# Seven block products in place of eight for the first products of the last 768 tokens

## Chip, cores and metric

The kernel runs on one core of a Trainium2 chip. The metric is the device time of one execution in microseconds; lower is better. The core has five engines with queues of their own: TensorE (PE, its weight loads as PEld), VectorE (DVE), ScalarE (ACT), GpSimd (POOL) and SyncE (SP), which here issues the DMAs.

## What is computed

Top-32 attention for 4 batches of 8 heads over 576 tokens, then two feed-forward layers on all 2304 tokens, in fp32.

```python
scores = scale * np.matmul(q, k.transpose(0, 1, 3, 2))
kth = np.partition(scores, -top_k, axis=-1)[..., -top_k:-top_k + 1]
...
x = np.ascontiguousarray(attn_out.transpose(0, 2, 1, 3)).reshape(B * S, H * D)   # 2304 x 512
x = (lambda h: np.maximum(0.01 * h, h) @ w_out)(x @ w_in)                       # 512 -> 2048 -> 512
h = x @ moe2_w_in
g = np.where(h >= 1, h, np.where(h <= -1, 0.0, (h + 1) ** 2 / 4.0))
out = g @ moe2_w_out
```

## The kernel before

Every feed-forward product is made of three matmuls (`mm3`, lines 829 to 832): an fp32 operand is held as a rounded part and a remainder (`split`, line 397: a cast on ACT, a subtraction on POOL), and high by high, high by low and low by high are added in one PSUM bank. Weights are split once, early in the kernel, and kept in DRAM (`scr`); `load_w` (line 495) brings one 128 x 2 x 512 tile of 512 KB into one of six `ring` buffers.

The program is written as a list of operations with dependences, and `Plan` (line 79 on) puts them in order at build time: it plays the list with a cost and a priority for every operation, lets every engine take the first operation that is ready and has its buffers, and emits the instructions in that order. So each engine's order is fixed before the run. `close` (line 90) adds an operation that waits for all operations on a set of tiles and then frees their memory for others: here those of the weight preparation (`EARLY`) for those of later attention (`LATE`).

Attention goes unit by unit (`unit_out`, line 988). When a block of tokens is done, `split_x` (line 820) splits it, and `FLOW` (line 36) says which blocks go through which layer (`ffn`, line 936). The last two entries are the last 768 tokens: the two blocks of 256 of batch 3, and the 4 x 64 remainders of all batches (`"r"`, tile `xr`). For 512 tokens `hidden` (line 853) makes the first product of one chunk of 128 of the 2048 hidden values at 512 columns, and for `"r"` two chunks at 256 columns; activation and split follow; `sums` (line 886) adds the second product in banks kept for the whole layer, two steps later. In the first layer the second product has the weights as the stationary operand and tokens as columns, in the second layer the activations are stationary and the 512 outputs are the columns. TensorE's feed-forward work comes after attention's in priority, so a backlog of it remains when attention ends.

## Time and profile before

| | us |
|---|---|
| median of 3 runs | 1185.3 (1185.26 to 1187.74) |
| the profiled execution | 1185.56 |
| its span in the trace | 1183.8 |
| TensorE busy in it | 1131.7 |
| Vector, Scalar, GpSimd busy | 869.9, 843.0, 710.2 |

The span is from the first to the last instruction in the trace. Recorded durations of matmuls overlap, since they are pipelined; how fast they follow one another is read from their starts. PEclk is the granted share of TensorE's full clock. A line number can be that of a helper, so tiles are named with it: `x` are split tokens, `gt` split activations, `t` and `gr` activation buffers, `ring` weights, `bank` PSUM banks.

### The profile page before, as it was taken

How to read it: one execution, taken by the hardware profiler on the slowest of the kernel's cores; microseconds unless marked ns; L12 is line 12 of the kernel's file. 1: busy time of each engine (PE TensorE's matmuls, PEld its weight loads, DVE VectorE, ACT ScalarE, POOL GpSimd, SP SyncE). 2: the span in 40 equal slices, each digit the busy share in tenths (PEclk: the TensorE clock that was granted, in tenths of full speed). 3: DMA queues.
4: the chain of work that ended last, by engine and by line, in shares of the span. 5: the costliest groups of instructions: out<-in, count | busy, mean ns of one | idle time of the engine just before them, and what ended most of it. 6: DMA issues, size and time to landing. Idle time of an engine off the chain costs nothing.

```text
span 1183.8 us, 18889 instructions
## 1 busy us (share of the span) xinstructions
PE 1131.7 (96%) x6240; PEld 966.1 (82%) x6240; DVE 869.9 (73%) x1761; ACT 843.0 (71%) x1889; POOL 710.2 (60%) x820
## 2 busy tenths in 40 slices
PE   6778898998999999999999999999999999999998
PEld 4566697997888888888888888888888888888887
DVE  7999999997999999999999999989961000012221
ACT  6888899997999989889877999888553212142223
POOL 3445588986979878677866678768462322252221
PEclk8988999999999999999999999999999999999999
DMA  9888798589658555545555564443546343233322
GB/s 343 283 301 298 234 368 323 204 314 383 231 199 285 181 196 171 199 155 196 192 198 175 171 202 150 136 142 121 175 147 197 136 143 114 100 142 143 137 100 102
DMA packets 78322, 236.45 MB, mean 200 GB/s; under 512 B 8720, under 2 KB 21136, under 8 KB 74128
## 3 DMA queue, kind: packets, MB, share of 16 engines
q1 hardware_dynamic: 78224, 235.24, 57.4%
q8 instruction: 49, 0.80, 0.3%
q14 instruction: 49, 0.40, 0.1%
HBM read 192.22 MB, written 42.99 MB: 199 GB/s over the span
## 4 chain that ended last, share of the span: by engine, by line
PE 72%; ACT 9%; DVE 8%; POOL 7%; issue 2%; DMA 1%; SPq 0%; POOLq 0%; ACTq 0%; DVEq 0%
PE bank L830 14%; PE bank L831 14%; PE bank L832 14%; PE bank L698 5%; PE bank L902 5%; PE bank L903 5%; PE bank L904 5%; PE bank L672 5%; DVE m L618 4%; PE bank L570 3%; DVE wk L622 3%; POOL px L390 2%; ACT e L640 2%; PE bank L718 2%; POOL e L657 1%
## 5 line engine op out<-in xcount | busy, mean ns | idle before, releaser
L390 POOL TENSOR_TENSOR gt<-gr,gt 128x512 fp32r<-128x512 f32 x144 | 187.8, 1304 | 256.2 <-ACT gt L374 132.8
L618 DVE MAX8 m<-wk 128x8 f32<-128x576 f32 x432 | 309.4, 748 | 0.5
L878 DVE TENSOR_SCALAR t<-bank 128x512 f32<-128x512 f32 x72 | 49.5, 687 | 237.5 <-POOL x L390 142.7
L622 DVE MATCH_REPLACE8 wk<-m,wk 128x576 f32<-128x576 f32 x288 | 212.6, 744 | 0.0
L830 PE MATMUL bank<-x,ring 128*128 128x512 f32 (+1 forms) x568 | 207.6, 366 | 0.3 <-DVE gr L881 0.3
L832 PE MATMUL bank<-x,ring 128*128 128x512 f32 (+1 forms) x568 | 202.3, 356 | 0.0
L831 PE MATMUL bank<-x,ring 128*128 128x512 f32 (+1 forms) x568 | 202.2, 356 | 0.0
L672 PE MATMUL bank<-idt,e 128*116 128x128 f32 (+1 forms) x720 | 110.4, 281 | 16.5 <-POOL e L657 9.4
L376 ACT ACTIVATE t<-t,half 128x512 f32<-128x512 f32 x72 | 52.2, 725 | 102.1 <-DVE t L878 102.1
L390 POOL TENSOR_TENSOR pt<-ptr,pt 116x512 fp32r<-116x512 f32 (+1 forms) x96 | 106.0, 1126 | 29.4 <-ACT pt L374 21.8
L657 POOL TENSOR_SCALAR e<-e,rc 128x576 f32<-128x576 f32 x144 | 111.6, 784 | 16.0 <-DVE rc L655 14.4
L832 PEld LDWEIGHTS bank<-x,ring 128*128 128x128 f32 x568 | 107.3, 189 | 15.7
L374 ACT COPY ptr<-bank 116x512 f32<-116x512 f32 (+1 forms) x224 | 106.4, 511 | 18.4 <-PE bank L672 15.9
L672 PEld LDWEIGHTS bank<-idt,e 128*116 128x116 f32 (+1 forms) x720 | 85.9, 138 | 40.0 <-POOL e L657 17.5
L830 PEld LDWEIGHTS bank<-x,ring 128*128 128x128 f32 x568 | 107.5, 189 | 12.2 <-DVE gr L881 0.9
L376 ACT ACTIVATE gt<-bank 128x512 fp32r<-128x512 f32 x72 | 43.2, 600 | 103.4 <-PE bank L832 103.0
L831 PEld LDWEIGHTS bank<-x,ring 128*128 128x128 f32 x568 | 107.7, 190 | 10.3
L618 DVE MAX8 m<-s 128x8 f32<-128x576 f32 x144 | 104.2, 747 | 8.6 <-ACT s L374 8.4
L376 ACT ACTIVATE e<-s,nb 128x576 f32<-128x576 f32 x144 | 108.4, 777 | 1.4
L830 PE MATMUL bank<-gt,ring 128*128 128x512 f32 (+1 forms) x304 | 109.3, 360 | 0.0
L374 ACT COPY s<-bank 128x288 f32<-128x288 f32 x256 | 96.1, 403 | 17.1 <-PE bank L570 15.7
L832 PE MATMUL bank<-gt,ring 128*128 128x512 f32 (+1 forms) x304 | 106.8, 351 | 0.0
(97 smaller groups left out, 2812.4 us busy)
## 6 DMA issues: line engine op xcount, KB each, us to landing
ring<-scr SPq DMA_DIRECT2D x212, 512.0 KB, 3.5
scr<-px SPq DMA_DIRECT2D x58, 512.0 KB, 4.9
wraw<-in_moe_w_in_dram SPq DMA_DIRECT2D x16, 1024.0 KB, 7.0
wraw<-in_moe_w_out_dram SPq DMA_DIRECT2D x16, 1024.0 KB, 7.4
kraw<-in_km_dram SPq DMA_DIRECT2D x40, 288.0 KB, 4.6
vl<-in_vd_dram SPq DMA_DIRECT2D x24, 320.0 KB, 5.8
qraw<-in_qm_dram SPq DMA_DIRECT2D x24, 256.0 KB, 3.9
vl<-in_vp_dram SPq DMA_DIRECT2D x16, 320.0 KB, 3.7
```

Source lines behind the costliest of these rows:

```text
L374: nc.scalar.copy(out=out_(), in_=in_())
L376: nc.scalar.activation(out=out_(), in_=in_(), func=func, **a)
L390: lambda: nc.gpsimd.tensor_tensor(out=out_(), in0=in0(), in1=in1(), op=ALU.subtract),
L618: vec(lambda i=i, c=c, src=src: nc.vector.max(out=m()[:, i, c], in_=src()), 664, [(m, (i, r))], [src], pr)
L622: vec(lambda i=i, c=c, src=src, w=ws[i]: nc.vector.match_replace(out=w(), in_to_replace=m()[:, i, c], in_values=src(), imm_value=NEG), 720 ...
L657: P.op("P", T_NORM, lambda i=i: nc.gpsimd.tensor_scalar(out=es[i](), in0=es[i](), scalar1=rc()[:, i:i + 1], scalar2=1.0, op0=ALU.mult, op1 ...
L672: nc.tensor.transpose(ps()[0:p, i * 128:(i + 1) * 128], e()[:, cols[j]], idt())
L698: nc.tensor.matmul(out_ps()[:, 0:w], lhsT=vt()[0:p, j, :], rhs=pt()[0:p, c] if lean else pt()[0:p, part, c], start=bi == 0 and part == 0 a ...
L830: nc.tensor.matmul(ps, lhsT=wh, rhs=xh, start=first, stop=False, skip_group_check=True)
L831: nc.tensor.matmul(ps, lhsT=wh, rhs=xl, start=False, stop=False, skip_group_check=True)
L832: nc.tensor.matmul(ps, lhsT=wl, rhs=xh, start=False, stop=last, skip_group_check=True)
L902: nc.tensor.matmul(acc[z](), lhsT=gh[:, c], rhs=wo()[:, 0], start=st, stop=False)
```

## The change

The last two entries of `FLOW` are replaced by `ffn_wide`. The 768 tokens stay in one tile `xr` and are seen as two halves of 384; the 512 features as two halves of 256; the hidden chunks as pairs (even, odd). For each pair, the 2 x 2 x 2 block product of tokens, features and chunks is made in seven products instead of eight (the Winograd form): `operands` makes the seven token operands from sums and differences (four sums for each of two feature chunks, fourteen splits), once a layer; `weights` makes four sums of weight blocks for each pair (two additions on POOL, four on DVE, two splits). The results are put together in four banks: ACT copies the bank of the first product to a second bank, on which TensorE then adds further products, and DVE adds the product kept in `p5` to it twice between two of them (`both`). `bend` is the activation.

Activations of the first half of the tokens (`g0`) are split at once and go into second sums, which are issued between the products of the next pair in the numbers of `FILL`. Those of the second half (`g1`) are kept unsplit for the whole layer; `late_split` splits them later, and their second sums follow when all eight pairs are through, with the second weights loaded a second time. These late sums end with the last three pairs taken bank by bank. The matmuls of `sums` are the same as before, at 384 columns in the first layer and 512 in the second. In the second layer the first two pairs do their first two products, which need the first half of the tokens alone, ahead of the others.

A third stage of memory is opened when all attention is done (`third`): the tiles in `LAST` take the place of those in `ATT` and `LATE`, and no operation on them starts earlier. The storage of old `x` and `gt` tiles is used again for late activations and split weight sums. Costs in the planner for the new operations are separate functions (`t_aa`, `t_pp`, `t_vv`). The diff, cut:

```diff
-LATE = ("vv", "vraw", "pt", "xb", "xr")
+LATE = ("vv", "vraw", "pt", "xb")
+ATT = ("xraw", "kk", "vl", "kraw", "qraw", "qh", "s", "wk", "e", "m8", "nb", "y", "sums", "rc", "ptr")
+BYVEC = (3, 4)
+TAIL = 3
+FILL = (((0, 0, 0, 0), (2, 2, 2, 2), (2, 2, 2, 2)), ((0, 0, 0, 0), (0, 0, 0, 3), (2, 2, 2, 1)))
+L_EARLY = 1
+EARLY_AT = ((0, 6, 2, 4), (1, 0, 3, 2))
+LAST = dict(xa=1, g0=2, g1=8, t0=2, u7=1, p5=2, tsn=2, wf=2, tf=2, ring2=4, cc=2)
+WORK = dict(gd=4, ts=5)
...
+    def load_w(key, prio, tag="ring"):
...
-        wt = new("ring", [128, 2, DM], F32R)
+        wt = new(tag, [128, 2, DM], F32R)
...
+    last = ((B - 1, 0), (B - 1, 1), "r")
+    x_raw = {}
...
+    def third():
+        late.close()
+        att.close()
+        for tag in LAST:
             pools[tag] = ctx.enter_context(tc.tile_pool(name="p_" + tag, bufs=1))
...
+        def product(self, ps, o, name, begin):
+            wt, k0 = self.w[name]
+            xa = self.wide.xa
+            for k in range(2):
+                def mm(k=k):
+                    c = slice((k0 + k) * 128, (k0 + k + 1) * 128)
+                    mm3(ps()[:, 0:HW], wt()[:, 0, c], wt()[:, 1, c], xa()[:, o, 0, k], xa()[:, o, 1, k], begin and k == 0, k == 1)
+                pe(mm, 3 * t_m(HW), [ps], [(xa, ((o, k), 0)), (xa, ((o, k), 1)), wt], fprio())
+        def bend(self, e, z, src, sref, psum):
+            hi, n, L, g0, r0, g1 = -5.0, HW, self.L, self.g0, self.r0, self.g1
+            dst, dref = (lambda: r0[e](), [r0[e]]) if z == 0 else (lambda: g1()[:, e], [(g1, e)])
+            if L == 0:
+                if z == 0:
+                    slope(lambda: g0()[:, e, 0], src, t_aa(n, psum), 0.01, [(g0, (e, 0))], sref, hi)
+                slope(dst, src, t_aa(n, psum), 0.01, dref, sref, hi)
+            else:
+                act(dst, src, t_aa(n, psum), dref, sref + [half1], hi, func=ACTF.Relu, scale=0.5, bias=half1)
+                act(dst, dst, t_aa(n), dref, dref, hi, func=ACTF.Square)
+                vec(lambda: nc.vector.scalar_tensor_tensor(out=dst(), in0=src(), scalar=1.0, in1=dst(), op0=ALU.max, op1=ALU.min),
+                    t_v(n) + 90 if psum else t_vv(n), dref, sref + dref, hi)
+                if z == 0:
+                    act(lambda: g0()[:, e, 0], dst, t_aa(n), [(g0, (e, 0))], dref, hi)
+            if z == 0:
+                sub(lambda: g0()[:, e, 1], dst, lambda: g0()[:, e, 0], n, [(g0, (e, 1))], dref + [(g0, (e, 0))], hi, t_pp)
+        def both(self, dst, w):
+            vec(lambda: nc.vector.tensor_tensor(out=dst(), in0=self.zb()[:, 0:HW], in1=self.p5(), op=ALU.add),
+                t_v(HW) + 90, w, [self.zb, self.p5], -6.0)
...
+        def open(self):
+            pb = lambda ps: (lambda: ps()[:, 0:HW])
+            self.product(self.za, 0, "b11", True)
+            act(pb(self.zb), pb(self.za), t_aa(HW, True), [self.zb], [self.za], -6.0)
+        def corner(self):
+            self.product(self.za, 1, "b21", False)
+            self.bend(0, 0, lambda: self.za()[:, 0:HW], [self.za], True)
+        def rest(self, fill, opened):
+            za, ze, zb, zc, u7 = self.za, self.ze, self.zb, self.zc, self.u7
+            pb = lambda ps: (lambda: ps()[:, 0:HW])
+            counts = FILL[self.L][min(self.i, 2)]
+            def chunk(k):
+                for _ in range(counts[k]):
+                    if fill:
+                        fill.pop(0)()
+            self.product(ze, 3, "t1", True)
+            act(self.p5, pb(ze), t_aa(HW, True), [self.p5], [ze], -5.5)
+            if not opened:
+                self.open()
+            chunk(0)
+            self.product(zb, 4, "t2", False)
+            self.both(pb(zc), [zc])
+            if not opened:
+                self.corner()
+            chunk(1)
+            self.product(zb, 5, "t3", False)
+            self.both(u7, [u7])
+            self.product(zc, 6, "b22", False)
+            self.bend(1, 0, pb(zc), [zc], True)
+            chunk(2)
+            self.product(zb, 2, "t4", False)
+            self.bend(1, 1, u7, [u7], False)
+            self.bend(0, 1, pb(zb), [zb], True)
+            chunk(3)
...
+        def weights(self, i):
+            hi = -6.0 + i if self.L == 0 and i < 1 else 40.0 + i if i < 2 else 100.0 + i
+            L = self.L
+            we, wo = (load_w((L, 2 * i + e, 0), fprio(), "ring2" if L == 0 and i == 0 else "ring") for e in range(2))
+            n = 2 * 128
+            full = []
+            for w in (we, wo):
+                f = new("wf", [128, 512])
+                P.op("P", t_pp(512), lambda f=f, w=w: nc.gpsimd.tensor_tensor(
+                    out=f(), in0=w()[:, 0].bitcast(F32), in1=w()[:, 1].bitcast(F32), op=ALU.add), w=[f], r=[w], prio=hi)
+                full.append(f)
+            fe, fo = full
+            ta, tb = (new("tf", [128, 512]) for _ in range(2))
+            for dst, z, a, za, b, zb, op in (
+                (ta, 0, fo, 0, fe, 0, ALU.subtract), (ta, 1, fo, 1, fo, 0, ALU.subtract),
+                (tb, 0, ta, 1, fe, 0, ALU.add), (tb, 1, fe, 1, tb, 0, ALU.subtract),
+            ):
+                vec(lambda dst=dst, z=z, a=a, za=za, b=b, zb=zb, op=op: nc.vector.tensor_tensor(
+                    out=dst()[:, z * n:(z + 1) * n], in0=a()[:, za * n:(za + 1) * n], in1=b()[:, zb * n:(zb + 1) * n], op=op),
+                    t_vv(n), [(dst, z)], [a if a not in (ta, tb) else (a, za), b if b not in (ta, tb) else (b, zb)], hi)
+            ts = []
+            for t in (ta, tb):
+                x = P.tile("ts", ts_make, "ts", (0, 1) if L == 0 and i == 0 else None)
+                split(lambda a, x=x: x()[:, a], t, 512, x, [t], 0, hi, t_pp, t_aa)
+                ts.append(x)
+            self.w[i] = dict(b11=(we, 0), b21=(we, 2), b22=(wo, 2), t1=(ts[0], 0), t3=(ts[0], 2), t2=(ts[1], 0), t4=(ts[1], 2))
...
+            for k in range(2):
+                cut(0, k, src(k, 0))
+            for k in range(2):
+                cut(1, k, src(2 + k, 0))
+            for k in range(2):
+                a11, a12, a21, a22 = src(k, 0), src(2 + k, 0), src(k, 1), src(2 + k, 1)
+                s1, s2, s3, s4 = tmp(c0, 0, k), tmp(c0, 1, k), tmp(c1, 0, k), tmp(c1, 1, k)
+                add(s3, a11, a21, ALU.subtract, True)
+                if self.L:
+                    act(lambda k=k: xr()[:, k, HW:], a21[0], t_aa(HW, True), [(self.xo, (k, 1))], a21[1], hi)
+                    a21 = (lambda k=k: xr()[:, k, HW:], [(self.xo, (k, 1))])
+                add(s1, a21, a22, ALU.add, True)
+                cut(3, k, s1)
+                add(s2, s1, a11, ALU.subtract)
+                cut(4, k, s2)
+                cut(5, k, s3)
+                add(s4, a12, s2, ALU.subtract)
+                cut(6, k, s4)
+                cut(2, k, a22)
...
+        def late_split(self, i):
+            g1 = self.g1[i]
+            gd = self.gd[i] = P.tile("gd", gd_make)
+            lo = 50.0 + i
+            act(lambda: gd()[:, :, 0], g1, t_aa(2 * HW), [(gd, (e, 0)) for e in range(2)], [g1], lo)
+            sub(lambda: gd()[:, :, 1], g1, lambda: gd()[:, :, 0], 2 * HW, [(gd, (e, 1)) for e in range(2)], [g1] + [(gd, (e, 0)) for e in range(2)], lo, t_pp)
...
+        def second_weights(self, i, tag="ring2"):
+            return [load_w((self.L, 2 * i + e, 1), fprio(), tag) for e in range(2)]
...
+        n = NF // 2
+        places = [((6, 7, 4, 5), (0, 1, 2, 3), (6, 7, 4, 5)), ((0, 1, 2, 3), (4, 5, 6), (7, 0, 1))]
+        nxt = Wide(0, xr, parts, places[0])
+        nxt.weights(0)
+        xo = Fixed(None, None, None, "xr")
+        xo.make = lambda: xr()
+        for L in range(2):
+            me = nxt
+            na = 4 if L == 0 else 3
+            me.xo = xo
+            fill = []
+            for i in range(n):
+                if i == 0:
+                    me.operands()
+                if L == 1 and i == 0:
+                    me.weights(1)
+                    early = [Pair(me, j) for j in range(2)]
+                    for p in early:
+                        p.open()
+                        p.corner()
+                if L == 1 and i < 2:
+                    early[i].rest(fill, True)
+                else:
+                    Pair(me, i).rest(fill, False)
+                if i + 1 < n and (L == 0 or i):
+                    me.weights(i + 1)
+                ws = me.second_weights(i)
+                fill += [go for e in range(2) for go in me.sums(i, me.g0[i], ws, me.acc, range(na), e)]
+            for go in fill:
+                go()
+            if L == 0:
+                me.out(0)
+            else:
+                me.out(0)
+            me.dacc = [bank(among=(z,), fifo=f"acc{z}") for z in me.db]
+            for i in range(n):
+                me.late_split(i)
+            if L == 0:
+                nxt = Wide(1, xo, lambda ks, z: [(k, z) for k in ks], places[1])
+            ws = {}
+            for i in range(n):
+                ws[i] = me.second_weights(i, "ring" if i == n - 1 else "ring2")
+                if i < n - TAIL:
+                    for e in range(2):
+                        for go in me.sums(i, me.gd[i], ws[i], me.dacc, range(na), e):
+                            go()
+            if L == 0:
+                nxt.weights(0)
+            for z in (0, 2, 1, 3) if L == 0 else range(na):
+                for i in range(n - TAIL, n):
+                    for e in range(2):
+                        for go in me.sums(i, me.gd[i], ws[i], me.dacc, (z,), e):
+                            go()
+            if L:
+                me.out(1)
+            else:
+                nxt.banks = me.dacc
...
-    flow = list(FLOW)
...
+    flow = list(FLOW[:-2])
...
     def unit_out(i):
         st_out(st.pop(i), float(i))
+        if i == len(units) - 1:
+            P.close(third)
+            ffn_wide()
+            return
         for g in blocks:
-            if done[g] == i:
+            if done[g] == i and g not in last:
...
```

## Rows read from the trace of the kernel before

**Rows 1.** the page: busy us (share); 40 slices, in tenths

```profile
PE 1131.7 (96%) x6240; PEld 966.1 (82%) x6240; DVE 869.9 (73%) x1761; ACT 843.0 (71%) x1889; POOL 710.2 (60%) x820
...
PE   6778898998999999999999999999999999999998
```

**Rows 2.** busy time in stretches of 100 us (columns in its first line)

```profile
core 0: us, PE busy (x) PEld busy (x) DVE busy (x) ACT busy (x) POOL busy (x), PEclk, DMA share, GB/s
0.00:100.00 100.00, 71.00 (x293) 53.87 (x294) 91.97 (x199) 82.91 (x192) 42.84 (x65) 0.89 0.87 307
...
300.00:400.00 100.00, 98.89 (x487) 81.31 (x485) 98.53 (x180) 94.44 (x194) 85.28 (x87) 1.00 0.67 230
...
1000.00:1100.00 100.00, 99.70 (x550) 86.97 (x549) 14.15 (x21) 28.57 (x53) 31.72 (x30) 1.00 0.35 127
```

**Rows 3.** timeline of ACT, POOL, DVE: start, duration, what [idle before]

```profile
883.56 0.42 ACT L374 COPY xr<-bank 64x64 f32<-64x64 f32 x2 [0.54 <-PE bank L725]
...
866.42 1.81 POOL L390 TENSOR_TENSOR gt<-gr,gt 128x512 fp32r<-128x512 f32 x1
...
892.06 1.30 POOL L390 TENSOR_TENSOR gt<-gr,gt 128x512 fp32r<-128x512 f32 x1 [4.42 <-ACT gt L374]
897.50 1.30 POOL L390 TENSOR_TENSOR gt<-gr,gt 128x512 fp32r<-128x512 f32 x1 [4.14 <-ACT gt L374]
...
889.03 0.69 DVE L878 TENSOR_SCALAR t<-bank 128x512 f32<-128x512 f32 x1 [3.40 <-PE bank L832]
```

**Rows 4.** timeline of TensorE, from three stretches

```profile
888.60 0.39 PE L832 MATMUL bank<-x,ring 128*128 128x512 f32 x1
...
913.31 0.39 PE L830 MATMUL bank<-x,ring 128*128 128x512 f32 x1
...
918.75 0.28 PE L830 MATMUL bank<-x,ring 128*128 128x256 f32 x1
...
921.50 0.28 PE L832 MATMUL bank<-x,ring 128*128 128x256 f32 x1
...
1046.58 0.40 PE L830 MATMUL bank<-x,ring 128*128 128x512 f32 x1
...
1051.82 0.39 PE L832 MATMUL bank<-x,ring 128*128 128x512 f32 x1
```

**Rows 5.** the chain that ended last, 850 to 1184: start, duration, what

```profile
1051.76 0.70 DVE gr L881
1052.51 0.39 PE bank L830
...
1179.42 0.59 ACT t L374
```

**Rows 6.** groups by form from 900 on: xcount | busy us, mean ns

```profile
L390 POOL TENSOR_TENSOR gt<-gr,gt 128x512 fp32r<-128x512 f32 x50 | 64.5, 1291 | 198.1 <-ACT gr L376 100.3 <-ACT gt L374 97.0 <-PE bank L832 0.8
...
L830 PEld LDWEIGHTS bank<-x,ring 128*128 128x128 f32 x260 | 49.3, 190 | 6.2 <-DVE gr L881 0.7
...
L881 DVE TENSOR_TENSOR gr<-bank,t 128x512 f32<-128x512 f32 x26 | 18.0, 692 | 22.6 <-ACT t L376 22.6
...
L374 ACT CAST gt<-gr 128x512 fp32r<-128x512 f32 x26 | 16.1, 621 | 23.0 <-DVE gr L881 21.7 <-PE bank L904 1.2
...
L390 POOL TENSOR_TENSOR x<-t,x 128x256 fp32r<-128x256 f32 x12 | 8.5, 752 | 2.2 <-ACT x L374 2.1
...
L374 ACT CAST x<-t 128x256 fp32r<-128x256 f32 x12 | 4.2, 407 | 0.1
```

**Rows 7.** Vector on tile wb: ns min/median/max, first and last start

```profile
L473 DVE SCALAR_TENSOR_TENSOR wb<-wa,wb x48: 667/748/1786, 136.1 to 405.0; 128x512 int32<-128x512 int32 x48
```

**Rows 8.** the old first layer's stretch; landing of ring loads

```profile
913.30:1046.50 133.20, 133.20 (x769) 118.06 (x768) 0.00 (x0) 31.31 (x62) 34.37 (x29) 1.00 0.38 132
...
DMA to landing us min/median/max: 3.1/3.9/5.5
```

**Rows 9.** Scalar's groups by form, whole span

```profile
L376 ACT ACTIVATE bank<-wraw 128x512 f32<-128x512 f32 x16 | 10.5, 656 | 0.7 <-DMA wraw<-in_moe_w_in_dram 0.6
```

More of the change, by code (lines that the diff above doesn't have):

```diff
@@ L86, in __init__ @@
         self.queue = {}
-        self.early = []
-        self.gate = None
+        self.before = [(EARLY, []), (ATT + LATE, [])]
+        self.behind = [LATE + ("xr",), tuple(LAST)]
+        self.gates = []
     def close(self, fn):
-        self.ops.append(("X", 0, fn, 0.0, set(self.early), [], []))
-        self.gate = len(self.ops) - 1
+        self.ops.append(("X", 0, fn, 0.0, set(self.before[len(self.gates)][1]), [], []))
+        self.gates.append(len(self.ops) - 1)
     def tile(self, tag, make, fifo=True, among=None):
@@ L127, in op @@
         refs = [x[0] if isinstance(x, tuple) else x for x in list(r) + list(w) + list(also)]
-        if any(x.tag in EARLY for x in refs):
-            assert self.gate is None
-            self.early.append(i)
-        if any(x.tag in LATE for x in refs):
-            deps.add(self.gate)
+        for z in range(2):
+            if any(x.tag in self.before[z][0] for x in refs):
+                assert len(self.gates) <= z
+                self.before[z][1].append(i)
+            if any(x.tag in self.behind[z] for x in refs):
+                deps.add(self.gates[z])
         self.ops.append((eng, ns, fn, prio, deps, new, refs))
@@ L976, in ffn, with __init__ @@
             r.out()
-    flow = list(FLOW)
+    class Pair:
+        def __init__(self, wide, i):
+            self.wide, self.i, self.L = wide, i, wide.L
+            self.w = wide.w.pop(i)
+            places = wide.pb if L_EARLY != wide.L or i > 1 else EARLY_AT[i]
+            self.za, self.ze, self.zb, self.zc = (bank(among=(z,), fifo=f"acc{z}") for z in places)
+            self.g0 = wide.g0[i] = new("g0", [128, 2, 2, HW], F32R)
+            self.g1 = wide.g1[i] = new("g1", [128, 2, HW])
+            self.r0 = [new("t0", [128, HW]) for _ in range(2)]
+            self.u7 = new("u7", [128, HW])
+            self.p5 = new("p5", [128, HW])
+        def product(self, ps, o, name, begin):
[59 more added lines that the diff above has]
+            chunk(3)
@@ L999, in unit_out @@
                     ffn(grps, L)
-                    if len(prep_last) == total and P.gate is None:
+                    if len(prep_last) == total and not P.gates:
                         P.close(second)
```

131 lines of the change are left out of this document (110 added, 21 removed).

## Prediction

> **What bounds the kernel now.** I read the engine shares and slices first. TensorE is busy 96% of the span, and after the first quarter all its slices read 9 [rows 1]. Only the opening, where VectorE leads, leaves TensorE idle; the stretches of 100 us say the same, at full clock (1.00) [rows 2]. So after about 300 us the end is a sum of TensorE work, and a change there is worth what it takes from that sum, less any new idle time. I then bounded the stage that the change replaces. The last attention work is the copy into xr that begins at 883.56 [rows 3]. TensorE's backlog at that point is the second layer of batch 2; the first product of the last 768 tokens begins at 913.31, their second layer at 1046.58, and the last evacuation starts at 1179.42 [rows 4, 5]. The stretch is 1179.42 - 913.31 = 266.1 us, with one idle moment of some 0.46 us (1051.82 plus one interval, to 1052.51) [rows 4, 5]. Vector and Scalar stand mostly idle there and GpSimd is a third busy [rows 2]: room for the added sums. The profiled execution took 1185.56 us for a span of 1183.8; the median of the three runs, 1185.3, lies 0.3 lower.
>
> **Rates.** Recorded durations overlap, so I use start-to-start. At 512 columns 24 intervals take 918.75 - 913.31 = 5.44 us, 0.2267 each; at 256 columns 23 intervals take 921.50 - 918.75 = 2.75 us, 0.1196 each [rows 4]. The new width, 384, is not in the trace. It lies between these ends; a line through both gives 0.173, which I take: 0.1071 for 256 columns leaves 0.0125 besides the columns at both ends. A check: the first layer before is 2 x (192 x 0.2267 + 192 x 0.1196) = 133.0 against 133.3 seen.
>
> **TensorE's part.** A pair of 128-wide chunks of the hidden width takes seven products of 2 x 3 matmuls, 42 matmuls of 384 columns; eight pairs are 336, or 58.1 us, in each layer. The classical form costs 192 x (0.2267 + 0.1196) = 66.5. The second sums keep their columns: in the first layer 8 x 2 x 4 x 3 = 192 matmuls of 384 for each half of the tokens, 384 in all, 66.4 us; in the second 288 of 512, 65.3 us, as before. Sum: 124.5 + 123.4 = 247.9 us against 266.1, 18.2 less; the drain behind the last matmul, some 0.2, stays, so **18.0 less** if TensorE never waits.
>
> **What is added elsewhere.** Eviction and splitting at 384 columns, halfway between the 256 and 512 rows: GpSimd 1.02 us, Scalar 0.51 [rows 6]. A pair in the steady part gives GpSimd two weight sums and two weight splits at 1.29, two activation splits at 1.02, and sooner or later a late split of 768 columns (1.8 by the same slope): 9.0 us of the pair's TensorE time of 7.27 + 24 x 0.173 = 11.4. Scalar in the second layer has twelve passes of about 0.5 and two casts of 0.62, 7.3 us. Both lie beside TensorE. Vector adds four 256-wide sums over two SBUF inputs, two bank sums and, in layer two, four blends. Their cost has bounds: a 512-wide evacuation is 0.692 [rows 6], a 512-wide operation with two SBUF inputs runs 0.667 to 1.786 [rows 7]; for 256 columns I take 0.42 when nothing blocks it and up to 1.1 more when GpSimd is reading. The median is 0.748, so at least half of such operations ran nearly unheld. Vector's total is 4 to 9 us a pair, hidden too.
>
> This is where the Trainium skill speaks against the change. The rows show the spread just named, and one GpSimd split of 1.81 us where its fellows take 1.29 [rows 3]. "SBUF — State Buffer", section "Who interferes with whom", says a Vector instruction with two SBUF inputs and a GpSimd instruction that reads SBUF exclude each other, the second waiting for the whole of the first. By that GpSimd's 9.0 us would grow by Vector's 4 x 0.42 to 10.7, still under 11.4; no more than a wait of that length shows in these rows, so the trace agrees as far as it goes.
>
> **Loads.** Each layer fetches its second weights twice: 16 more loads of 512 KB per layer, 32 in all. Beside steady pairs four loads fall in 11.4 us, about 184 GB/s, and in the late sums 16 in 33 us, about 254, plus four early ones of the next layer. The 16 engines moved 307 GB/s at a share of 0.87 in the first 100 us [rows 2], and 132 at 0.38 here [rows 8]. A load lands after 3.1 to 5.5 us [rows 8]; a tile is used for 2.08 us, so four late buffers turn round in 4 x 2.08 = 8.3 us, against some 3.9 + 2.1 + 0.3 = 6.3 needed. Hidden, except where the last three pairs are kept: pair 6 waits for buffers freed in pair 4, 2 us before the tail. I price that 0.4 per layer, bounds 0 to 2.
>
> **The new gate and its queues.** The third pool close waits for all attention work, 883.56 + 0.42, and TensorE has backlog until 913.3, so 29 us cover it. Behind that gate SP holds two weight loads; behind those on the same queue stand ring loads of batch 2, protected by six buffers. GpSimd then has five batch-2 splits (1.29 each, one every 5.4 us [rows 3]), the first pair's weights (four at 1.29) and twelve operand cuts at 1.02: 23.9 us, done by about 908, or 915 if Vector's fourteen operations with two SBUF inputs (some 7 us) all exclude it. The seventh product needs its operand only 6 us after 913. The removed splits of batch 3 and of the remainders (12 pairs on Scalar and GpSimd) cost TensorE nothing and return nothing. The second pair's weights add 5.2 + 1.7, to 921, when TensorE wants them at 921.3: cover gone, so 0 to 4, I take 1.
>
> **Hand-overs inside a pair.** A bank's last matmul begins at 888.60 [rows 4], its interval ends at 888.83, and Vector starts at 889.03 [rows 3]: 0.20. From Vector to TensorE it is 0.05 (1051.76 + 0.70 to 1052.51) [rows 5]. The first product is copied by Scalar from bank to bank: no such row; nearest are 0.656 for 512 columns written into a bank [rows 9] and 0.407 for 256 between SBUF tiles [rows 6], I take 0.50. That is 0.75 us between the first product and the second that accumulates on it. Two fill sums (1.04) cover it in later pairs; the first pair has no fill and pays **0.8**. The bank sum (0.57 + 0.25 = 0.82) stands behind a product of 1.04 in the first layer. In the second layer's two early pairs that product has gone ahead, so up to 0.82 each is bare. From the last late sum to the second layer's third product: bank sum 0.57, cast 0.51, split 1.02, hand-overs 0.3, 2.4 us, under four early products of 1.04. For this whole hand-over I take 1.5, bounds 0 to 4.
>
> **Sum.** 18.0 - 0.8 - 1.0 - 2 x 0.4 - 1.5 = 13.9 off 1185.56, 1171.7; against the median 1171.4. With every term at its bounds the losses are 0 to 13, so 1167 to 1180.
>
> **Rivals.** (a) *Helpers trail in the unfilled places*: the weights of pairs 1 and 2 and both hand-overs are late, each by 3 to 4 us, losses of 8 to 16: about 1178. For it: low priority of those sums, chains across four engines. Against: idle helpers [rows 2]. (b) *Weight sums become the bound, slower than before*: the sums of a pair run load, GpSimd, Vector, Scalar, GpSimd, through two buffers each. With every GpSimd and Vector step held once: 4 x 1.29 + 4 x (0.42 + 1.1) + 4 x 1.0 + 0.6 = 15.9 us if nothing of the next pair overlaps; overlapped, the front half sets the pace, 2 x 2.3 + 4 x 1.52 = 10.7. It decides once a pair takes more than 11.4 + 13.9/14 = 12.4. Halfway, 13.3, costs 14 x 1.9 = 27: 1198. Against it: the median of [rows 7], and that TensorE ran at 98.9 of 100 us with GpSimd 85% and Vector 99% busy [rows 2]. (c) *The seven products don't cost seven eighths*: a 128-wide weight load is recorded at 190 ns [rows 6]; were it exposed at 384 columns, 1056 x (0.190 - 0.173) = 18 us, all of the gain: 1185. Against it: 256-wide matmuls follow at 0.1196 with the same loads [rows 4].
>
> **How the numbers follow.** Forecast 0.68, (a) 0.17, (b) 0.07, (c) 0.03, and 0.05 for a gain beyond the sum (the earlier order shifting a little). What a measurement can tell from no change is 0.2%, 2.4 us. Faster: 0.68 + 0.17 + 0.05 = 0.90; same: (c) and 0.01 of (b), 0.04; slower: the other 0.06 of (b). Range: from the loss-free sum, 1167, to 1181, past the upper bound by the better half of (a).
>
> **What would show it.** Starts of 384-wide matmuls 0.173 apart; about 720 and 336 of them; the first near 913; late sums 33 us long with TensorE full; TensorE idle after 913 of 3 to 5 us, found before the second accumulated product, at the second pair, at the layer's change. Wrong if pairs repeat every 12 us or more with TensorE waiting on a GpSimd split, if the start is behind 916, or if DMA landing grows past 6 us in the late sums.

## The result, and the profile after

The changed kernel takes 1172.59 us (median of 4, 1170.99 to 1177.45) where the kernel before takes 1186.16 (median of 4, 1185.26 to 1187.74): a ratio of 0.9891, 95% interval 0.9859 to 0.9923: 1.1% faster, well outside the interval. A second set gave 1172.69 us and 0.9875 (0.9852 to 0.9897). The profiled execution took 1170.99 us for a span of 1169.2, against 1185.56 for 1183.8 before: 14.6 us less. In two of the experiments, the changed kernel repeated and the doubled Vector sums, the profiled execution was disturbed (2714 and 1267 us), so of these two the other executions' times are used and no trace.

The page of the changed kernel, its engine shares and two of its rows of slices (busy tenths, 40 slices); it answers to [rows 1]:

```profile
PE 1117.1 (96%) x6144; PEld 973.2 (83%) x6144; DVE 937.7 (80%) x1862; ACT 893.9 (76%) x2005; POOL 805.1 (69%) x884
...
PE   6778898999999999999999999999999999999998
...
POOL 3445588886879878676866767778558885659721
```

From the eighth slice on TensorE's read 9, the last excepted. GpSimd, a third busy in this part before [rows 2], is now busy for most of it. The same by stages, busy us of each engine in stretches of the changed kernel (steady pairs of the first layer, its late sums, pairs of the second layer, its late sums); it answers to [rows 2, 8]:

```profile
core 0: us, PE busy (x) PEld busy (x) DVE busy (x) ACT busy (x) POOL busy (x), PEclk, DMA share, GB/s
...
929.00:1002.00 73.00, 73.00 (x423) 73.00 (x422) 21.62 (x37) 33.09 (x69) 49.62 (x42) 1.00 0.56 187
1002.00:1036.00 34.00, 34.00 (x196) 33.66 (x195) 2.55 (x6) 8.65 (x16) 16.27 (x13) 1.00 0.66 206
1036.00:1134.00 98.00, 98.00 (x515) 91.38 (x514) 53.95 (x81) 62.49 (x125) 66.06 (x52) 1.00 0.52 178
1134.00:1166.00 32.00, 30.74 (x136) 24.92 (x134) 0.00 (x0) 5.11 (x7) 7.35 (x4) 1.00 0.64 221
```

TensorE is busy for the whole of 73, 34 and 98 us at a granted clock of 1.00; GpSimd is the next fullest with 68% of the steady pairs. So the end is still a sum of matmuls. Its beginning and end, as TensorE's timeline around the first new product (start us, duration, engine, line, operation, tiles, shapes, idle time before and releaser), which answers to [rows 4]:

```profile
913.82 0.39 PE L955 MATMUL bank<-ring,gt 128*128 128x512 f32 x1
914.05 0.33 PE L881 MATMUL bank<-xa,tsn 128*128 128x384 f32 x1
...
915.11 0.33 PE L881 MATMUL bank<-xa,ring 128*128 128x384 f32 x1
...
915.98 0.34 PE L883 MATMUL bank<-xa,ring 128*128 128x384 f32 x1
916.87 0.44 PE L881 MATMUL bank<-xa,tsn 128*128 128x384 f32 x1 [0.55 <-ACT bank L400]
...
1040.03 0.33 PE L881 MATMUL bank<-xa,ring 128*128 128x384 f32 x1
```

and as the last two pieces of the chain that ended last (start us, us), which answer to [rows 5]:

```profile
1164.52 0.24 PE bank L1231
1164.82 0.59 ACT t L400
```

Six products of 384 columns take 915.11 - 914.05 = 1.06 us with the two that are a little slow, and six in the steady part 1.04: 0.1733 apart. The first begins at 914.05 (913.31 before), the second layer at 1040.03 (1046.58), the last evacuation at 1164.82 (1179.42). So the replaced stretch lasts 250.77 us instead of 266.11, 15.34 less, and it begins 0.74 later: 14.6, the whole of the difference between the two spans. The late start lies ahead of the change's own work: between 650 and 914 us TensorE now waits 0.5 us once on the split of e by GpSimd (L683), where before it waited for nothing. The 4800 matmuls ahead of the first new product are the same in both kernels and in the same order up to the 3778th; from there on the planner has put them in another order.

All that TensorE waits for after 880 us by its waits (engine, line, waited for: us in total, times, longest; idle times up to 0.15 us are not listed) is one line, the copy of the first bank in the first pair:

```profile
PE bank L881 <- ACT bank L400: 0.6, 1, 0.6
```

So 2.6 us of the 18.0 are not had: 0.72 at that copy (915.98 plus an interval, to 916.87), 0.7 in small pieces over the rest of the first layer (1040.03 - 914.05 = 125.98 against 720 x 0.173 = 124.6), and 1.2 in the second (1164.82 - 1040.03 = 124.79 against 123.4 and the drain of 0.2), most of which the section on the hardware below finds at changes of width.

### The profile page after: what moved, and what is told of

The parts are those of the page before. It is cut to its first block, busy times and chain, and to the rows that moved or that the text cites. A ratio compares the mean times of both kernels' runs of the same rounds, so it can differ in the third digit from the quotient of the medians.

```text
span 1169.2 us, 19068 instructions
## 1 busy us (share of the span) xinstructions
PE 1117.1 (96%) x6144; PEld 973.2 (83%) x6144; DVE 937.7 (80%) x1862; ACT 893.9 (76%) x2005; POOL 805.1 (69%) x884
## 4 chain that ended last, share of the span: by engine, by line
PE 73%; ACT 10%; DVE 8%; POOL 5%; issue 2%; DMA 1%; SPq 0%; POOLq 0%; ACTq 0%; DVEq 0%
PE bank L881 14%; PE bank L882 14%; PE bank L883 14%; PE bank L724 5%; PE bank L698 5%; DVE m L644 4%; PE bank L596 4%; PE bank L953 3%; PE bank L955 3%; PE bank L954 3%; DVE wk L648 3%; PE bank L1231 2%; PE bank L1230 2%; PE bank L1229 2%; ACT e L666 2%
## 5 line engine op out<-in xcount | busy, mean ns | idle before, releaser
L416 POOL TENSOR_TENSOR gt<-gr,gt 128x512 fp32r<-128x512 f32 x96 | 126.7, 1320 | 45.8 <-ACT gt L400 23.5
L881 PE MATMUL bank<-x,ring 128*128 128x512 f32 (+2 forms) x376 | 142.8, 380 | 0.0
L883 PE MATMUL bank<-x,ring 128*128 128x512 f32 (+2 forms) x376 | 137.6, 366 | 0.0
L882 PE MATMUL bank<-x,ring 128*128 128x512 f32 (+2 forms) x376 | 137.6, 366 | 0.0
L683 POOL TENSOR_SCALAR e<-e,rc 128x576 f32<-128x576 f32 x144 | 112.2, 788 | 19.5 <-DVE rc L681 18.5
L400 ACT COPY s<-bank 128x288 f32<-128x288 f32 x256 | 95.9, 402 | 18.2 <-PE bank L596 16.6
L648 DVE MATCH_REPLACE8 wk<-m,s 128x576 f32<-128x576 f32 x144 | 106.2, 742 | 0.0
L666 ACT ACTIVATE e<-e,nb 128x576 f32<-128x576 f32 x130 | 100.9, 778 | 4.0 <-POOL nb L659 3.4
L416 POOL TENSOR_TENSOR px<-wb,px 128x512 fp32r<-128x512 f32 x58 | 76.1, 1320 | 28.8 <-ACT px L400 23.1
L596 PE MATMUL bank<-kk,qh 128*128 128x288 f32 x384 | 84.0, 312 | 2.2 <-ACT xraw L400 1.1
L724 PE MATMUL bank<-ptr,vl 116*128 116x256 f32 (+1 forms) x320 | 78.3, 390 | 2.2 <-ACT ptr L400 2.0
L883 PEld LDWEIGHTS bank<-x,ring 128*128 128x128 f32 x376 | 70.8, 188 | 10.7
L881 PEld LDWEIGHTS bank<-x,ring 128*128 128x128 f32 x376 | 70.9, 189 | 6.5 <-DMA ring<-scr 0.2
L882 PEld LDWEIGHTS bank<-x,ring 128*128 128x128 f32 x376 | 71.1, 189 | 5.2
```

What stands on the lines that cost most here:

```text
L400: nc.scalar.copy(out=out_(), in_=in_())
L416: lambda: nc.gpsimd.tensor_tensor(out=out_(), in0=in0(), in1=in1(), op=ALU.subtract),
L596: nc.tensor.matmul(ps()[:, 0:HALF], lhsT=qh()[:, at] if plain else qh()[:, part, at], rhs=kk()[:, c * HALF:(c + 1) * HALF], start=(i == 0) ...
L648: vec(lambda i=i, c=c, src=src, w=ws[i]: nc.vector.match_replace(out=w(), in_to_replace=m()[:, i, c], in_values=src(), imm_value=NEG), 720 ...
L666: P.op("A", 763, lambda i=i: nc.scalar.activation(out=es[i](), in_=es[i](), func=ACTF.Exp, bias=nb()[:, i, 2:3], accum_out=sums()[:, i:i + ...
L683: P.op("P", T_NORM, lambda i=i: nc.gpsimd.tensor_scalar(out=es[i](), in0=es[i](), scalar1=rc()[:, i:i + 1], scalar2=1.0, op0=ALU.mult, op1 ...
```

## The experiments

All are edits of the changed kernel; costs are against its 1172.69 us unless said otherwise. They ran on several chips, on which the kernel before had medians of 1185.76 to 1187.21 us, so one microsecond between two of them is not resolved. An edit that the planner sees also moves the attention work a little: the first new product begins between 911.98 and 919.76 us in the traces, so where it matters the stretch from there to the last evacuation is given too (250.77 us in the changed kernel).

**The changed kernel again**, as the common measure.

> The changed kernel as it is, on the same chip as the next three, as their base. Theory (the gain is TensorE's columns): 1170 to 1174 us, TensorE's 384-wide matmuls start 0.173 apart, one wait of some 0.6 us in the first pair. Rival (the time came from an accident of one chip): a time away from 1171 to 1174 by more than 4 us.

1172.69 us, ratio 0.9875 (0.9852 to 0.9897).

**Eight products instead of seven.** The gain should be the columns of the eighth product and nothing else.

```diff
             self.product(ze, 3, "t1", True)
+            self.product(ze, 3, "t1", True)
```

> Each pair makes the product with operand 3 twice in a row, the second over the first, so eight products per pair instead of seven, with everything else of the change as it is. Theory (the gain is the eighth product's columns): 16 pairs x 6 x 0.173 = 16.6 us more, about 1188 to 1190, a little above the kernel before. Rival (the gain comes from the new staging, of which the seven products are a small part, and helpers set the pace): the added matmuls fall into waiting time and the time grows by under 8 us, to 1180 or less.

1189.97 us, 17.3 more, ratio 1.0026 (1.0013 to 1.0038). The 96 added matmuls at 0.1733 are 16.6, and in the trace the stretch is 17.4 longer (1184.76 - 916.62 = 268.14). So the columns account for the gain. With eight products, the late sums and all the helpers' added work the kernel is 3.1 us slower than the kernel before; in the traces its stretch is 2.0 longer than the 266.11 before, and it begins 3.3 later.

**The first product of the first pair issued first**, so that its copy lies beside the next product.

```diff
             def chunk(k):
                 ...
+            if not opened and self.i == 0:
+                self.open()
             self.product(ze, 3, "t1", True)
             act(self.p5, pb(ze), t_aa(HW, True), [self.p5], [ze], -5.5)
-            if not opened:
+            if not opened and self.i:
                 self.open()
```

> In the first pair of the first layer the product that is copied from bank to bank is issued ahead of the first one instead of behind it, so that the copy lies beside 1.04 us of matmuls. Theory (the wait of 0.7 us is that copy's hand-over and nothing else): TensorE's wait there goes and no new one comes, 0.7 us less, 1170.3 to 1173. Rival (the operands of the third product are late there, whatever the order): TensorE still waits 0.5 us or more in the first pair, time unchanged.

TensorE's waits from 900 us on are now one:

```profile
PE bank L1231 <- DMA ring<-scr: 0.2, 1, 0.2
```

The wait for the copy is gone, so its cause was named rightly. The time, 1173.06 us (0.9883, 0.9858 to 0.9908), can't be told from 1172.69: 0.7 us is under what four runs resolve, and in the trace the stretch is 0.16 shorter (250.62), with a wait on a load that wasn't there before.

**No early products in the second layer.** The prediction put the layer's hand-over at 1.5 us with them.

```diff
-L_EARLY = 1
+L_EARLY = 9
...
-                    early = [Pair(me, j) for j in range(2)]
-                    for p in early:
-                        p.open()
-                        p.corner()
-                if L == 1 and i < 2:
-                    early[i].rest(fill, True)
+                    pass
+                if L == L_EARLY and i < 2:
+                    pass
```

> In the second layer no pair makes its first two products ahead of the others; all pairs are issued alike. Theory (the chain from the last late sum to the first product of the mixed operands, bank sum, cast, split, is bare for what the early products covered): the planner can still move one pair's two products ahead, 2.1 us against a chain of 2.4 and more splits behind it, so TensorE waits 0.5 to 3 us in all about the layer's change; 1172 to 1176. Rival (the operands are ready anyway, since the last late sums are taken bank by bank): no wait over 0.2 us there, 1171 to 1173.

1175.19 us, 2.5 more (0.9905, 0.9879 to 0.9931). TensorE's waits from 910 us on, the same columns:

```profile
PE bank L881 <- ACT bank L400: 1.1, 2, 0.6
PE bank L1229 <- DMA ring<-scr: 0.6, 1, 0.6
PE bank L1231 <- POOL g L416: 0.4, 1, 0.4
PE bank L881 <- DVE bank L1073: 0.2, 1, 0.2
```

The copy is bare a second time, and a bank sum and an activation split appear, all three between 1043 and 1059 us. That is the hand-over that was priced; in the changed kernel the early products hide all of it. The 0.6 us on a load lie at 1146, in the late sums, and don't belong to it.

**All second sums of a pair behind its last product**, so that nothing is put between the products by hand.

```diff
-FILL = (((0, 0, 0, 0), (2, 2, 2, 2), (2, 2, 2, 2)), ((0, 0, 0, 0), (0, 0, 0, 3), (2, 2, 2, 1)))
+FILL = (((0, 0, 0, 0), (0, 0, 0, 8), (0, 0, 0, 8)), ((0, 0, 0, 0), (0, 0, 0, 3), (0, 0, 0, 7)))
```

> The second sums of the pair before are issued all at the end of a pair instead of in four portions between its products. Theory A (the portions cover the copy from bank to bank and the bank sums): each of 7 pairs of the first layer and 6 of the second waits 0.7 after its copied product, 9 us more, about 1181. Theory B (the planner's own choice of the next ready operation fills these gaps whatever the list order): no wait over 0.2 us beside the first pair's, 1171 to 1174.

1173.82 us (0.9892, 0.9866 to 0.9918): 1.1 more, not resolved. The waits are the first pair's 0.6 and one of 0.2 on a load. The second theory on record holds: the planner finds covering work by itself, and the places written out by hand are not what hides the hand-overs.

**Only the last pair taken bank by bank in the late sums.**

```diff
-TAIL = 3
+TAIL = 1
```

> The late sums of a layer end with one pair taken bank by bank instead of three, so that all four banks of the first layer become ready within 2.1 us of its end instead of one each 3.1 us. Theory (taking three pairs bank by bank is what hides the second layer's operands): twelve more microseconds of GpSimd splits fall behind the end, with 4.2 us of early products and some of the pairs' other work before them: TensorE waits 1 to 5 us about the layer's change, 1173 to 1178. Rival (the early products alone are cover enough): no wait over 0.3 us there, 1171 to 1173.

1173.74 us (0.9896, 0.9869 to 0.9922), 1.0 more, with one added wait of 0.3 us on a bank sum. The theory of 1 to 5 us fell; the tail's form costs nothing that these runs can tell.

**GpSimd's weight additions doubled and tripled.** This is the rival that could have made the kernel slower: at which load of GpSimd do the weight sums set the pace? By the busy sum there were 2 us free in a pair, and a doubled addition adds 2 x 1.32 = 2.65.

```diff
+                for _ in range(2):      # tripled: range(3)
                     P.op("P", t_pp(512), lambda f=f, w=w: nc.gpsimd.tensor_tensor(
```

> As the run with three of each weight addition, with two: GpSimd gets 2.8 us more a pair. Theory (a pair lasts as long as GpSimd's whole list for it, late split included, once that is longer than TensorE's 11.4): 9.4 + 2.8 = 12.2, 0.8 over, 14 pairs make 11 us; two pairs' lead in each layer takes some back, so 1174 to 1186. Rival (late splits give way, so that 10.4 to 11.4 counts and nothing is over): 1171 to 1174, no waits on GpSimd.

> GpSimd makes each of a pair's two weight additions three times instead of once, so four more operations of some 1.39 us a pair, with the same result: 5.6 us on about 9.4, 15.0 us in all and 13.1 without the late split, against 11.4 us of TensorE a pair. Theory (GpSimd's work is hidden until its pair takes longer than TensorE's): about 13 pairs x 1.7 = 22 us, less the lead of two pairs of split weights in each layer (2 x 5 us), 8 to 22 us slower than the changed kernel, 1180 to 1194, and TensorE waits for a GpSimd split. Rival (helpers have so much room that TensorE never sees them): 1171 to 1175 and no waits.

Doubled: 1198.96 us, 26.3 more (1.0103, 1.0082 to 1.0124). Tripled: 1230.96, 58.3 more (1.0376, 1.0348 to 1.0403). Both expectations were far too small. TensorE's waits with three additions, from 900 us on, the first four lines:

```profile
PE bank L881 <- ACT bank L400: 9.3, 7, 2.6
PE bank L881 <- DVE bank L1073: 7.7, 12, 0.7
PE bank L1230 <- ACT g L400: 7.1, 4, 1.9
PE bank L883 <- POOL gt L416: 4.4, 4, 1.7
```

The work was added to GpSimd, but of all waits, some 35 us, nearly half are on Scalar's bank copy and on Vector's bank sum: hand-overs that don't use GpSimd at all. Over the 14 pairs behind each layer's first, 37 us of GpSimd time were added by each step, and the steps cost 26.3 and 32.0. With two additions GpSimd is busy 58.73 of the 71 us from 929 to 1000. Counted at every 42nd matmul of the products, pairs are 11.5 to 14.5 us apart in the first layer behind its first pair (12.8 at its end) instead of 11.4 to 11.5, and 14.3 to 17.2 in the second, from its third pair on, instead of 11.5 to 12.2.

**The same, with the late splits moved out of the way.** One theory was that GpSimd's list, its late splits included, sets the pace.

```diff
-            lo = 50.0 + i
+            lo = 500.0 + i
```

(with the doubled addition)

> Each weight addition twice as in the run that gave 1199 us, but the late splits have a lower priority than the weight sums instead of a higher one, so that they leave the steady pairs. Theory (GpSimd's list for a pair sets the pace: 11.9 us there, and pairs 12.8 apart): without the 1.87 of the late split it is 10.1 and under TensorE's 11.4, so most of the loss is gone: 1173 to 1180. Rival (the chain addition, sums, cast, split of one pair's weights sets the pace, whatever else GpSimd does): the late split is not on it, 1193 to 1200 as before.

1197.54 us, 24.9 more (1.0087, 1.0058 to 1.0117). The theory fell. GpSimd's timeline and TensorE's, between 972 and 992 us:

```profile
972.09 3.87 POOL L1138 TENSOR_TENSOR wf<-ring 128x512 f32<-128x512 f32 x3
977.22 0.99 POOL L416 TENSOR_TENSOR g<-t,g 128x384 fp32r<-128x384 f32 x1 [1.26 <-DVE tf L1147]
...
983.08 3.91 POOL L1138 TENSOR_TENSOR wf<-ring 128x512 f32<-128x512 f32 x3
990.02 1.01 POOL L416 TENSOR_TENSOR g<-t,g 128x384 fp32r<-128x384 f32 x1 [3.03 <-ACT t L402]
```

```profile
978.35 0.45 PE L881 MATMUL bank<-xa,ring 128*128 128x384 f32 x1 [1.07 <-ACT bank L400]
991.15 0.45 PE L881 MATMUL bank<-xa,ring 128*128 128x384 f32 x1 [1.07 <-ACT bank L400]
```

No late split falls here, GpSimd itself stands idle for 1.26 and 3.03 us, and still the pairs are 991.15 - 978.35 = 12.8 us apart. So a full GpSimd doesn't set the pace.

**The planner told other costs, nothing else changed.** Does another order by itself cost something?

```diff
 def t_vv(n):
-    return 1.3 * n + 650
+    return t_v(n)
 def t_aa(n, psum=False):
-    return t_a(n) + 60
+    return t_a(n, psum)
 def t_pp(n):
-    return 2.3 * n + 250
+    return t_p(n)
```

> The planner is told the old, lower costs for the new operations (a 512-wide GpSimd split 1.24 us instead of 1.43, a 256-wide Vector sum 0.33 instead of 0.98, a Scalar pass 0.06 less); the operations are the same. Theory (helpers run ahead of TensorE by more than such errors): same time, 1171 to 1175, no wait over 0.5 us beside the first pair's. Rival (the order of the queues is as close to the edge as the doubled additions showed): TensorE waits on Vector and GpSimd in most pairs, 1177 to 1195.

1187.14 us, 14.5 more (1.0011, 0.9998 to 1.0025): the whole gain gone, against the expectation of no change. Every instruction is still there, only in another order. That order is not one to use: splits of weight sums are written into the storage of old `gt` tiles at 915.72 and 917.60 us, before the last sums from `gt` tiles (919.53), and some of the results are different. Largest of TensorE's waits from 880 us on:

```profile
PE bank L881 <- ACT bank L400: 4.9, 4, 2.1
PE bank L955 <- POOL gt L416: 1.9, 1, 1.9
```

In the trace 5.7 us of the loss lie ahead of the first new product (919.76) and 10.0 in the stretch (260.81). So an order can cost as much as the change gains, and the doubled addition, which also changed the order, had not yet separated the two. Hence the next run.

**The addition doubled inside one planned step**, so that the planner sees the old cost and gives the order of the changed kernel on every engine.

```diff
-                P.op("P", t_pp(512), lambda f=f, w=w: nc.gpsimd.tensor_tensor(
-                    out=f(), in0=w()[:, 0].bitcast(F32), in1=w()[:, 1].bitcast(F32), op=ALU.add), w=[f], r=[w], prio=hi)
+                def twice(f=f, w=w):
+                    for _ in range(2):
+                        nc.gpsimd.tensor_tensor(
+                            out=f(), in0=w()[:, 0].bitcast(F32), in1=w()[:, 1].bitcast(F32), op=ALU.add)
+                P.op("P", t_pp(512), twice, w=[f], r=[w], prio=hi)
```

> Each weight addition is again made twice, but the planner isn't told: it sees one operation of the old cost, so that every engine has the order of the changed kernel and only GpSimd's real work is 2.65 us a pair longer. Theory (what made 1199 of the run in which the planner knew is the fixed order, in which TensorE's fill sums stand in other places and the bank copies lie bare; GpSimd itself was idle 1 to 3 us a pair there): GpSimd's list of 11.9 us is just over TensorE's 11.4, so 0 to 10 us slower than the changed kernel, 1172 to 1183. Rival (GpSimd's work itself is too long): 1190 to 1200 with this order too, TensorE waiting on GpSimd's splits.

1196.87 us, 24.2 more (1.0078, 1.0055 to 1.0101). In the traces the order is the changed kernel's on all four engines, instruction by instruction but for the added additions, so it is not the cause; GpSimd's added time is. The profiled execution is 25.9 longer: 3.0 ahead of the first new product (917.06) and 22.9 in the stretch (1190.71 - 917.06 = 273.65). The timeline of all engines around one wait shows how the added time gets to TensorE:

```profile
989.35 1.28 POOL L416 TENSOR_TENSOR gt<-tf,gt 128x512 fp32r<-128x512 f32 x1
989.42 1.49 DVE L1150 TENSOR_TENSOR tf<-wf,wf 128x256 f32<-128x256 f32 x1 [3.31 <-POOL wf L1139]
...
990.31 0.34 PE L883 MATMUL bank<-g,ring 128*128 128x384 f32 x1
990.59 1.17 POOL L416 TENSOR_TENSOR g<-t,g 128x384 fp32r<-128x384 f32 x1
990.84 1.21 DVE L1150 TENSOR_TENSOR tf<-wf 128x256 f32<-128x256 f32 x1
991.97 0.54 DVE L1073 TENSOR_TENSOR u<-bank,p 128x384 f32<-128x384 f32 x1
...
992.43 0.41 DVE L1150 TENSOR_TENSOR tf<-tf,wf 128x256 f32<-128x256 f32 x1
...
992.57 0.44 PE L881 MATMUL bank<-xa,tsn 128*128 128x384 f32 x1 [1.92 <-DVE u L1073]
```

Vector takes its instructions in the order in which they were emitted. Its queue holds a weight sum that waits 3.31 us for GpSimd's second addition, then two weight sums stretched to 1.49 and 1.21, and only behind these the bank sum at 991.97 that TensorE needs; TensorE, through with its product at 990.65, waits 1.92 us. The lengths follow GpSimd: the two long sums end at 990.91 and 992.05, each 0.28 to 0.29 us behind the end of a GpSimd split (990.63 and 991.76), and the one at 992.43, with GpSimd idle until its last 0.07 us, takes 0.41. Scalar's queue does the same at another place: a cast that waits for such a sum stands before the bank copies.

```profile
958.26 0.62 ACT L400 CAST gt<-tf 128x512 fp32r<-128x512 f32 x1 [3.30 <-DVE tf L1150]
...
959.15 0.48 ACT L400 COPY bank<-bank 128x384 f32<-128x384 f32 x1
...
959.69 0.44 PE L881 MATMUL bank<-xa,gt 128*128 128x384 f32 x1 [1.97 <-ACT bank L400]
```

Of TensorE's seven waits over 1.5 us in the stretch, six (at 921.70, 929.46, 959.69, 992.57, 1098.05 and 1111.25, 12.5 us together) have a weight sum or its cast, late by GpSimd, ahead of the hand-over in Vector's or Scalar's queue.

**Vector's weight sums doubled**, the mirror experiment.

```diff
+                for _ in range(2):
                     vec(lambda dst=dst, z=z, a=a, za=za, b=b, zb=zb, op=op: nc.vector.tensor_tensor(
```

> GpSimd as in the changed kernel; each of the four weight sums that Vector makes for a pair is made twice, so 4 x 0.77 = 3.1 us more of Vector a pair, with the same result. Theory (GpSimd's list sets the pace, and Vector only lengthens it by what it holds the shared reads, 4 x 0.42 = 1.7 us): 9.4 + 1.7 = 11.1 against 11.4, with some idle time of GpSimd between: 0 to 8 us slower, 1172 to 1181. Rival (the chain of a pair's weight sums sets the pace): 3.1 us longer is more than the 2.65 that made 1199, so 1195 to 1205.

1189.28 us, 16.6 more (1.0025, 1.001 to 1.0041), between the two theories' figures. Vector has a busy sum of 22 of 73 us in the changed kernel's steady pairs, and yet more of the same work costs 1.2 us a pair. That fits sums that stand in front of hand-overs, but it isn't shown, and there is a rival: the planner knew of the doubled sums and gave every engine another order, which by itself can cost as much (14.5 us above). The sums were not doubled in the old order.

## Why the prediction was right, and where its steps were not

- **TensorE's part held to a few tenths.** 18.0 us less if TensorE never waits, from a rate of 0.173 that no row showed; measured 0.1733. The eighth product put back costs 17.3 for 16.6 worked out. Rival (c), weight loads exposed at 384 columns, is out: it needed starts 0.190 apart.
- **First pair's copy: 0.8 predicted, 0.72 measured**, in the place named, and gone when the product is issued first.
- **Second pair's weights 1.0, tails 2 x 0.4, layer change 1.5: each nothing.** No wait stands at any of them, and of the 3 to 5 us of idle time forecast behind 913, 0.55 are seen. For the tails the loads were early enough: landing between 1002 and 1036 took 3.8 to 4.6 us (median 4.4), and the window shows 206 GB/s where 254 was estimated, since 13 loads were issued in it and not 20. At the layer's change the early products left nothing of the 1.5 us priced; without them the kernel is 2.5 us longer (3.6 by the two ratios to the kernel before). Rival (a), helpers that trail there, is thereby out.
- **Left out: 0.74 us of later start and about 1.9 us in small pieces.** Sum of the losses 3.3 instead of 4.1, so 14.6 in the profiled executions for 13.9 predicted, and 13.6 between the medians. That the total fits within 1 us is part luck: about 3 us of predicted waits are missing, and about 2.6 us of other losses stand in their place.
- **Rival (b) was the step that was mis-sized.** Its mechanism is real, though it doesn't act at this size, and the prediction's margin was a difference of busy sums, 11.4 - 9.0 = 2.4 us a pair. The list measured 9.4. The groups of the changed kernel from 884 us on (line, operation, tiles, count, busy us, mean ns, idle time before and releasers), which answer to [rows 6]:

```profile
L1137 POOL TENSOR_TENSOR wf<-ring 128x512 f32<-128x512 f32 x32 | 44.5, 1394 | 6.2 <-DMA ring<-scr 4.2 <-PE bank L955 0.9 <-POOL g L416 0.8
L416 POOL TENSOR_TENSOR g<-t,g 128x384 fp32r<-128x384 f32 x32 | 33.1, 1035 | 37.0 <-ACT t L402 14.4 <-PE bank L883 9.0 <-ACT g L400 8.4
L416 POOL TENSOR_TENSOR x<-g,x 128x768 fp32r<-128x768 f32 x16 | 29.9, 1867 | 23.1 <-ACT x L400 23.0
```

  With two splits of weights at 1.31 to 1.38 that is 2 x 1.39 + 2 x 1.35 + 2 x 1.035 + 1.87 = 9.4 us in 11.4. Of the 2.0 that seem free, the run with the addition doubled in the old order shows how much is: it adds 2.65 us a pair, 37 us in 14 pairs, and the stretch grows by 22.9, so 14.1/14 = 1.0 us a pair cost nothing. Of the 22.9, 4.8 are matmuls at the lower clock (see the section on the hardware); counted without them 1.4 us a pair were free. An estimate from these, if each microsecond beyond the free one costs a full one: even with the kernel before (13.5 us, 0.96 a pair) it would have been at some 2 us more a pair, a list of 11.4 us. The decision point was given as a pair of 12.4 us, and the doubled addition gave longer pairs, nearly all of 12.8 us or more, and a kernel slower than before, as this has it. The error was to put the pair's time equal to a list's sum: the list there is 9.4 + 2.65 = 12.05 at most, and pairs took up to 17.2, since the queues are in order and hold TensorE's own hand-overs too.
- **Vector's 256-wide sums: 0.42 free, up to 1.1 more, was nearly right.** Vector's operations on the tile of weight sums in the changed kernel (duration min, median, max in ns), which answer to [rows 7]:

```profile
L1146 DVE TENSOR_TENSOR tf<-wf,wf x16: 416/426/1507, 895.0 to 1102.0; 128x256 f32<-128x256 f32 x16
L1146 DVE TENSOR_TENSOR tf<-wf x16: 412/599/2054, 896.4 to 1102.3; 128x256 f32<-128x256 f32 x16
```

  The free time is as estimated from the 512-wide rows; the worst, 2.05, is 1.6 more. The Trainium skill's rule, "SBUF — State Buffer", section "Who interferes with whom", that such a Vector instruction and a GpSimd instruction that reads SBUF exclude each other for a whole instruction, agrees with the ends 0.28 to 0.29 us behind GpSimd's in the run with the addition doubled in the old order. By that rule GpSimd's list was to grow to 10.7; it grew to 9.4, as it was mostly Vector that came second. In the changed kernel 26 of Vector's 64 sums take over 0.6 us, all 26 end 0.28 us behind the end of a GpSimd instruction, and the 64 take 22.6 us more than at 0.42 each; GpSimd's groups of a pair take 6.9 more than at their shortest.

**What stays open:** how the waits behind the doubled addition divide between sums that start late (in-order waiting) and sums that are held; and what a layer wholly without late splits beside its pairs would show, since in the run that moved them four still fell between 932 and 965 us. Why Vector's doubled sums cost 16.6 us is open as well. No experiment gave a version faster than the changed kernel.

## What to carry to other kernels

Where the end is a sum of TensorE work, price an algebraic saving in columns at the start-to-start rate of the new width (16.6 us worked out, 17.3 when they were put back), and look for losses where nothing is left to fill a hand-over. The room on a helper is not its pair time less its busy sum: 2.0 us on paper were about 1 in fact, because an in-order queue puts work that isn't urgent ahead of the hand-over that TensorE waits for. And such a schedule is as fragile as its planner's costs: other costs for the same instructions took back 14.5 us.

## What the runs showed of the hardware that was not expected

**Where the width changes, a little is lost.** TensorE's timeline of the changed kernel in the second layer, where 384-wide products and 512-wide second sums alternate:

```profile
1057.22 0.33 PE L883 MATMUL bank<-xa,ring 128*128 128x384 f32 x1
1057.39 0.39 PE L1229 MATMUL bank<-ring,g 128*128 128x512 f32 x1
...
1058.09 0.33 PE L881 MATMUL bank<-xa,gt 128*128 128x384 f32 x1
...
1059.15 0.39 PE L1229 MATMUL bank<-ring,g 128*128 128x512 f32 x1
```

Three of 512 take 0.70 (0.68 at 0.2267), six of 384 take 1.06 (1.04 at 0.1733). Over the 44 stretches of one width from 1040 to 1128 us the surplus sums to 0.9 us, 0.02 each: most of the 1.2 us that the second layer lost with no wait. In the first layer, where the tiles change 83 times at one width, its 718 intervals lose 0.36 us in all, 0.02 of it at the changes. But in the second layer activations also become the stationary operand where the width changes, so it isn't shown that the width itself is the cause. With the second sums listed behind the last product the planner still made nearly as many changes, so what fewer would give wasn't tried.

**Waiting can cost a second time.** With the addition tripled, the stretch behind one wait of TensorE, first as a window (columns as above), then as TensorE's timeline:

```profile
1145.00:1148.50 3.50, 3.46 (x10) 3.17 (x11) 2.81 (x4) 1.07 (x3) 1.85 (x2) 0.51 0.04 6
```

```profile
1145.05 0.69 PE L881 MATMUL bank<-xa,ring 128*128 128x384 f32 x1 [2.62 <-ACT bank L400]
1145.53 0.52 PE L882 MATMUL bank<-xa,ring 128*128 128x384 f32 x1
1145.85 0.52 PE L883 MATMUL bank<-xa,ring 128*128 128x384 f32 x1
```

Behind a wait of 2.62 us the granted clock was 0.51, the 1.2 GHz level, and the matmuls came 0.32 us apart instead of 0.173 before it rose again. Matmuls in such places cost 10.5 us beyond their rates with three additions and 3.2 with two: that is part of why the third addition cost more, 32.0 us, than the second, 26.3. With the addition doubled in the old order it is 4.8 us, behind waits of 2.27, 1.97 and 1.95 us; the last of the three places as a window:

```profile
1111.50:1114.60 3.10, 3.10 (x10) 3.10 (x11) 2.08 (x3) 1.91 (x4) 3.02 (x3) 0.50 0.03 11
```

Behind three other waits of that run, of 2.37, 1.92 and 1.99 us, it stayed at 1.00. All stages of the changed kernel shown above ran at 1.00.
